# Own staging buffers for two chunks' k and q, first-layer weights fetched in pairs and held back, and new priorities, in a planned attention and MLP kernel

## The chip, the cores and the metric

The kernel runs on one core of one Trainium2 chip. The metric is the device time of one execution in microseconds (us). Three runs of the kernel before gave 1087.58, 1088.27 and 1089.88 us, a median of 1088.27 us.

## What is computed

The reference runs a delta-rule linear attention over 768 tokens (4 batches, 8 heads, head size 48), and sends its output, as 3072 tokens of 384 values, through two MLP layers with 2048 hidden units each:

```python
    for t in range(S):
        kt, vt, bt = (k_n[:, :, t], v[:, :, t], beta[:, :, t, None])
        y[:, :, t] = np.einsum('bhd,bhde->bhe', q[:, :, t], state)
        v_old = np.einsum('bhde,bhd->bhe', state, kt)
        state = state + bt[:, :, :, None] * np.einsum('bhd,bhe->bhde', kt, vt - v_old)
...
    h = x @ w_in          # layer 1: 0 below -1, h above 1, (h+1)^2/4 between; layer 2: h*clip(h+3,0,6)/6
    return (g @ w_out).astype(np.float32)
```

The MLP weights arrive as 64-bit floats, and the kernel must turn them into 32-bit ones.

## The kernel before

**Attention.** The 768 tokens are cut into 12 chunks of 64 (`c0` to `c11`). For each chunk `front(c)` loads k twice (`load_kv` into `KN`, `load_tok` into the staging tiles `ST0` and `ST1`), q (`load_tok`) and v (`load_v` into `E`), normalises k (`norms`), transposes k and q on TensorE through `ST` (`transposes`, L471), multiplies them (`products`), and inverts a triangular matrix for each head (`inverse`). The inverse is a chain of 15 small steps, each a multiply into `TMP` (L566) and a subtraction from `TL` (L571); in chunk 0 it runs on VectorE, in the others on GpSimd. Around the steps stand transposes on VectorE (L587 or L624 before, L604, L605, L620 and L633 behind) and four groups of 32x32 matmuls. `chain(c)` then takes the state through the chunk (matmuls `E,G`, then `E,KN`) and writes its output y (matmuls `KQ,E`), which is copied to `XB`; a last quarter of the rows goes by way of `YS` and six small DMAs (L786). Half `hb` 0 and half `hb` 1 of the heads are loaded and multiplied one after the other: with two staging tiles, the k and q of half 1 can be loaded only when the transposes of half 0 have read theirs.

**MLP.** Layer 1 works on blocks of tokens: chunk 0, chunk 1, and then pairs of chunks; layer 2 on six pairs. A block passes 16 slices `f` of the hidden units: 9 matmuls `XB,WL` (hidden values, called H here), an activation on ScalarE and VectorE (`GF`, `GH`, `GL`), and 9 matmuls `GH/GL,WL` (called O here). Values and weights are split into a high and a low part, hence three products each.

**Weights.** `wload` (L798) brings slice f: four DMAs of w_in and one of w_out, 768 KB in all, into one of four buffers `RAWL`, or for f 12 to 15 into a single `RAWR`. Then two halves (`pc` 0 and 1) are converted, each by three operations on VectorE (L826, L831, and the low part in L357), and by two or three on ScalarE (L366, L828, L366), into `WLA` or `WLB`. A buffer is loaded again once it has been read.

**The order.** Nothing is ordered by hand. `Plan` collects all operations with priorities from the table `PR`, and `emit` (L79) lays them out on the engines by its own estimate of durations; each engine then runs its list strictly in that order, and all DMAs are issued by SyncE (SP) in one list. A priority says which of several ready operations comes first. Up to the first MLP matmul, `emit` fills TensorE's free time with dummy matmuls (`bank<-GH`, 128x512; called fillers here):

```python
                while filling and x > filling:
                    d = 213.0 if is_warm(x) else 427.0
                    if x + d > t - 100.0:
                        break
```

Of the kernel before, what the change touches and what calls it, by code (L numbers as in the profile page):

```python
# [37 lines left out]
class Plan:  # L38
# [40 lines left out]
    def emit(self, banks, spare, fill):  # L79
# [54 lines left out]
        while todo:  # L134
# [3 lines left out]
            for e, lst in avail.items():  # L138
# [13 lines left out]
                for i in lst:  # L152
# [23 lines left out]
                if cand is not None and HOLD and e == "dve":  # L176
                    lim = cand[0] + HOLD
# [21 lines left out]
            if e == "pe":  # L199
# [70 lines left out]
def fused_kernel(  # L270
# [123 lines left out]
    P.op("act", 520, lambda: nc.scalar.activation(out=GH[0], in_=GF[0], func=AF.Copy, scale=1.0), r=[("gf", 0)], w=[("gh", 0)], prio=-30)  # L394
    for i in range(NST):
# [747 lines left out]
```

## Time and profile before

| | |
|---|---|
| median of three runs | 1088.27 us |
| the profiled execution: its time, and its span in the trace | 1090.76 us, 1089.0 us |
| TensorE matmuls (PE) busy | 1045.1 us, 96% |
| VectorE (DVE) busy | 662.6 us, 61% |
| ScalarE (ACT) busy | 595.7 us, 55% |
| GpSimd (POOL) busy | 277.6 us, 25% |
| granted TensorE clock, mean | 0.983 |

All rows below come from the one profiled execution, so sums are made against its 1090.76 us: its span and 1.76 us around it. PE's busy time holds the fillers and matmuls at the lower clock too, so 96% is not 96% of useful work. A granted clock of 1.00 is 2.4 GHz and 0.50 is 1.2 GHz.

### The profile page before, as it was taken

How to read it: one execution, taken by the hardware profiler on the slowest of the kernel's cores; microseconds unless marked ns; L12 is line 12 of the kernel's file. 1: busy time of each engine (PE TensorE's matmuls, PEld its weight loads, DVE VectorE, ACT ScalarE, POOL GpSimd, SP SyncE). 2: the span in 40 equal slices, each digit the busy share in tenths (PEclk: the TensorE clock that was granted, in tenths of full speed). 3: DMA queues.
4: the chain of work that ended last, by engine and by line, in shares of the span. 5: the costliest groups of instructions: out<-in, count | busy, mean ns of one | idle time of the engine just before them, and what ended most of it. 6: DMA issues, size and time to landing. Idle time of an engine off the chain costs nothing.

```text
span 1089.0 us, 25916 instructions
## 1 busy us (share of the span) xinstructions
PE 1045.1 (96%) x10684; PEld 890.1 (82%) x10684; DVE 662.6 (61%) x1258; ACT 595.7 (55%) x1164; POOL 277.6 (25%) x652
## 2 busy tenths in 40 slices
PE   8985899999999999999999999999999999999998
PEld 6764888887777778778778788898999998999897
DVE  4969778777869767786855589533333333333332
ACT  4768686766668576765755689433323232322322
POOL 3022313084755858548460000000000000000000
PEclk9987899999999999999999999999999999999999
DMA  9963243231314303322122284402011020200000
GB/s 179 191 142 66 61 99 66 45 63 36 59 21 97 69 17 59 90 45 46 40 57 83 80 257 139 116 1 88 1 41 47 1 87 2 59 29 1 29 1 29
DMA packets 174757, 71.86 MB, mean 66 GB/s; under 512 B 121264, under 2 KB 170544, under 8 KB 174640
## 3 DMA queue, kind: packets, MB, share of 16 engines
q1 hardware_dynamic: 174640, 70.22, 27.1%
q8 instruction: 84, 1.38, 0.6%
q14 instruction: 33, 0.27, 0.1%
HBM read 53.68 MB, written 14.16 MB: 62 GB/s over the span
## 4 chain that ended last, share of the span: by engine, by line
PE 72%; DVE 11%; ACT 5%; DMA 4%; POOL 3%; issue 3%; SPq 1%; DVEq 0%; POOLq 0%; ACTq 0%
PE bank L389 71%; DMA RAWL<-in_moe_w_in_dram 2%; DVE X L506 2%; POOL TL L571 1%; POOL TMP L566 1%; ACT KQ L514 1%; DVE GF L880 1%; PE bank L471 1%; DVE KQ L535 1%; DMA RAWR<-in_moe_w_in_dram 1%; DVE GL L357 1%; DVE DL L624 1%; ACT G L366 1%; SPq L815 1%; DVE XB L777 1%
## 5 line engine op out<-in xcount | busy, mean ns | idle before, releaser
L389 PE MATMUL bank<-XB,WLA 128*128 128x512 f32 (+1 forms) x1404 | 341.2, 386 | 13.4 <-DMA XB<-YS 7.1
L389 PEld LDWEIGHTS bank<-XB,WLA 128*128 128x128 f32 x1404 | 251.9, 193 | 62.1 <-ACT TBS L828 6.6
L357 DVE TENSOR_TENSOR GL<-GF,GH 128x512 fp32r<-128x512 f32 (+1 forms) x208 | 139.4, 671 | 82.9 <-PE bank L389 57.4
L884 DVE SCALAR_TENSOR_TENSOR GF<-GF,bank 128x512 f32<-128x512 f32 x96 | 66.1, 688 | 193.0 <-ACT GF L883 192.9
L366 ACT ACTIVATE GH<-GF 128x512 fp32r<-128x512 f32 (+1 forms) x202 | 120.9, 599 | 114.3 <-DVE GF L884 69.1
L883 ACT ACTIVATE GF<-bank 128x512 f32<-128x512 f32 x96 | 57.5, 599 | 204.5 <-PE bank L389 203.6
L566 POOL TENSOR_TENSOR TMP<-TL,DL 128x126 f32<-128x126 f32 (+25 forms) x293 | 113.0, 386 | 115.8 <-DVE DL L624 65.7
L571 POOL TENSOR_TENSOR TL<-TL,TMP 128x126 f32<-128x126 f32 (+25 forms) x293 | 126.6, 432 | 23.0
L389 PE MATMUL bank<-GH,WLA 128*128 128x512 f32 (+1 forms) x504 | 121.5, 373 | 2.6 <-DVE GH L368 1.5
L389 PE MATMUL bank<-XB,WLB 128*128 128x512 f32 (+1 forms) x468 | 112.4, 382 | 0.2 <-DVE GF L880 0.2
L389 PE MATMUL bank<-WLA,GH 128*128 128x384 f32 x576 | 112.3, 336 | 0.0
L389 PEld LDWEIGHTS bank<-WLA,GH 128*128 128x128 f32 x576 | 102.8, 188 | 6.4
L389 PEld LDWEIGHTS bank<-GH,WLA 128*128 128x128 f32 x504 | 85.9, 192 | 20.7 <-ACT GH L366 3.5
L389 PEld LDWEIGHTS bank<-XB,WLB 128*128 128x128 f32 x468 | 83.4, 191 | 15.5 <-DVE GF L880 0.4
L880 DVE SCALAR_TENSOR_TENSOR GF<-bank,GF 128x512 f32<-128x512 f32 (+1 forms) x112 | 68.6, 612 | 45.0 <-ACT GF L879 43.8
L878 ACT ACTIVATE GF<-bank 128x512 f32<-128x512 f32 (+1 forms) x112 | 59.8, 534 | 60.6 <-PE bank L389 56.1
L389 PE MATMUL bank<-GL,WLA 128*128 128x512 f32 (+1 forms) x252 | 65.9, 370 | 0.0
L879 ACT ACTIVATE GF<-GF 128x512 f32<-128x512 f32 (+1 forms) x112 | 63.5, 567 | 2.4
L389 PE MATMUL bank<-WLA,GL 128*128 128x384 f32 x288 | 61.5, 334 | 0.0
L389 PEld LDWEIGHTS bank<-WLA,GL 128*128 128x128 f32 x288 | 51.0, 188 | 0.0
L389 PE MATMUL bank<-GH 128*128 128x512 f32 x176 | 50.8, 437 | 0.0
L389 PEld LDWEIGHTS bank<-GL,WLA 128*128 128x128 f32 x252 | 43.9, 191 | 8.2 <-issue 0.3
(135 smaller groups left out, 1357.6 us busy)
## 6 DMA issues: line engine op xcount, KB each, us to landing
XB<-X SPq DMA_DIRECT2D x36, 256.0 KB, 4.7
X<-XB SPq DMA_DIRECT2D x30, 256.0 KB, 2.6
KN<-in_k_dram SPq DMA_DIRECT2D x24, 192.0 KB, 4.0
ST<-in_k_dram SPq DMA_DIRECT2D x48, 96.0 KB, 3.1
ST<-in_q_dram SPq DMA_DIRECT2D x48, 96.0 KB, 3.3
E<-in_v_dram SPq DMA_DIRECT2D x24, 192.0 KB, 3.8
RAWL<-in_moe_w_out_dram SPq DMA_DIRECT2D x12, 384.0 KB, 4.2
KQ<-in_moe_w_in_dram SPq DMA_DIRECT2D x12, 384.0 KB, 5.2
```

Source lines behind the costliest of these rows:

```text
L357: alts[e] = (d, lambda e=e: ENG[e].tensor_tensor(out=val(out), in0=val(in0), in1=val(in1), op=op))
L366: lambda: nc.scalar.activation(out=val(out), in_=val(in_), func=AF.Copy, scale=scale))
L389: nc.tensor.matmul(o, l, r, start=start, stop=stop)
L471: nc.tensor.transpose(bk.tile[0:112, p * 128:(p + 1) * 128], ST[i][:, p, 0:112], IDN)
L506: P.op("dve", 335, lambda bk=bk, u0=u0, rr=rr, ro=ro: nc.vector.tensor_tensor(out=X[rr, u0:u0 + NP, :], in0=bk.tile[ro].rearrange("p (a x) ...
L566: P.op(te, d, lambda t=t, s=s, r0=r0, a0=a0, a1=a1, m=m: ve.tensor_tensor(out=t[:, a0:a1], in0=TL[:, r0 + a0:r0 + a1, s:s + 1].to_broadcas ...
L571: P.op(te, d, lambda t=t, s=s, r0=r0, a0=a0, a1=a1: ve.tensor_tensor(out=TL[:, r0 + a0:r0 + a1, 0:s], in0=TL[:, r0 + a0:r0 + a1, 0:s], in1 ...
L878: P.op("act", da, lambda: nc.scalar.activation(out=gf, in_=ps, func=AF.Relu, scale=0.5, bias=0.5), r=[hkey(hb)], w=[gk], prio=MP)
L879: P.op("act", da + 48, lambda: nc.scalar.activation(out=gf, in_=gf, func=AF.Square), w=[gk], r=[gk], prio=MP)
L880: P.op("dve", 1.06 * n + 60, lambda: nc.vector.scalar_tensor_tensor(out=gf, in0=ps, scalar=1.0, in1=gf, op0=ALU.max, op1=ALU.min), r=[hkey ...
L883: P.op("act", da, lambda: nc.scalar.activation(out=gf, in_=ps, func=AF.Relu, scale=1.0 / 6.0, bias=0.5), r=[hkey(hb)], w=[gk], prio=MP)
L884: P.op("dve", 1.06 * n + 60, lambda: nc.vector.scalar_tensor_tensor(out=gf, in0=gf, scalar=1.0, in1=ps, op0=ALU.min, op1=ALU.mult), r=[hke ...
```

## The change

- **Staging.** The list `ST` gets four more entries, which are not new tiles but parts of `G0` and `G1`, the tiles that hold the inverse. Half 1 of chunk 0 uses the two in `G0`, half 1 of chunk 1 the two in `G1`, and half 0 of both uses `ST0` and `ST1`. From chunk 2 on there are two as before. The four parts are zeroed first; the zeroing of `G` for its later use (`zero_g`) moves behind the products of chunks 0 and 1.
- **Weights.** `wload` takes a list of slices. The first twelve of layer 1 come in pairs: the same five DMAs move 1536 KB, with runs twice as long in w_in, into one of two buffers that are each as large as two were. A pair's buffer is free once both slices are converted. Slices 12 to 15 and layer 2 stay single.
- **Held back.** DMAs of layer 1's weights are marked `bulk`: the planner places one no earlier than 2.5 us before its own estimate of when the DMA engines are free.
- **The planner's numbers.** Seven priorities, a bias and a margin change; a filler counts 228 or 430 ns instead of 213 or 427, and must end 150 ns ahead of the next matmul instead of 100; short runs of a DMA count as more bytes.

```diff
-PR = dict(kv=-2.451, tok=-1.879, norm=-2.407, tr=-1.803, prod=-3.087, pm=-1.495, inv=-2.162, sv=-0.287, w=-1.124, chain=-0.022, y=-0.474,
-          wl=-0.036, wls=0.003, mp=0, lv=-0.894, first=3.58, bias=27.418, fill=3000, tpool=tuple(range(1, 12)), hc=2, halves=1, biasa=601.736, b16=(0, 1, 2, 3), hyst=4058, margin=800, umargin=300, urg=('inv', 's'), sw=(217, 95), ad=('act', 'dve'), dp=('dve', 'pool'), dg=('dve',), dw=('dve',), pq=190)
+PR = dict(kv=-2.566, tok=-1.879, norm=-2.601, tr=-1.803, prod=-3.087, pm=-0.932, inv=-2.162, sv=0.06, w=-1.449, chain=-0.205, y=-0.455,
+          wl=-0.036, wls=0.003, mp=0, lv=-0.894, first=3.58, bias=-148.421, fill=3000, tpool=tuple(range(1, 12)), hc=2, halves=1,
+          biasa=601.736, b16=tuple(range(0, 4)), hyst=4058, fgap=150, back=2500.0, dh=0, margin=753.154, umargin=300, urg=('inv', 's'),
...
+                    if o["bulk"]:
+                        t = max(t, dma_free - PR["back"])
...
+    gs = [G[i].rearrange("p u e s -> p (u e s)") for i in range(2)]
+    extra = [gs[0][:, 0:512], gs[0][:, 512:1024], gs[1][:, 1024:1536], gs[1][:, 1536:2048]]
+    ST += [x.rearrange("p (a x) -> p a x", a=NP) for x in extra]
...
-        i = stage[0] % NST
+        if c < 2:
+            i = (0 if hb == 0 else 2 + 2 * c) + stage[0] % 2
+        else:
+            i = stage[0] % NST
...
-    def wload(f, wi, wo, perm, prio, raw, rkey, tmps):
+    def wload(fs, wi, wo, perm, prio, raw, rkey, tmps):
...
+        if c < 2:
+            zero_g(c)
...
+    rawp = RAWL.rearrange("p (g i) c -> p g (i c)", i=2)
+    for g in range(NFA // 2):
+        wload([2 * g, 2 * g + 1], w1i, w1o, True, PR["wl"] + PR["wls"] * 2 * g, rawp[:, g % 2, :], ("raw", g % 2), tmps1)
```

What this does to the engines' lists shows in three places. The first is SP's list near the start, before; `KN`, `ST` and `E` are the k, q and v of chunks 0 and 1, `RAWL` the weights, and the two `ST` rows at the end are half 1 of chunk 0.

```order
L422 DMA KN_76<-in_k_dram 64x16x48 x2
L411 DMA ST_78<-in_k_dram 64x8x48 x2
L411 DMA ST_79<-in_q_dram 64x8x48 x2
L429 DMA E_71<-in_v_dram 64x16x48 x2
L422 DMA KN_77<-in_k_dram 64x16x48 x2
L815 DMA RAWL<-in_moe_w_in_dram 48x3x256
L815 DMA RAWL<-in_moe_w_in_dram 16x3x256
L815 DMA RAWL<-in_moe_w_in_dram 48x3x256
L815 DMA RAWL<-in_moe_w_in_dram 16x3x256
L411 DMA ST_78<-in_k_dram 64x8x48 x2
L411 DMA ST_79<-in_q_dram 64x8x48 x2
```

In the changed kernel there follow on the k and q of half 0 and the first half of v:

```order
L420 DMA G_74<-in_k_dram 64x8x48 x2
L420 DMA G_74<-in_q_dram 64x8x48 x2
L438 DMA E_71<-in_v_dram 64x16x48
L431 DMA KN_77<-in_k_dram 64x16x48 x2
L420 DMA ST_78<-in_k_dram 64x8x48 x2
L420 DMA G_75<-in_k_dram 64x8x48
L420 DMA ST_79<-in_q_dram 64x8x48 x2
L420 DMA G_75<-in_k_dram 64x8x48
L420 DMA G_75<-in_q_dram 64x8x48 x2
L438 DMA E_72<-in_v_dram 64x16x48 x2
L420 DMA ST_78<-in_k_dram 64x8x48 x2
L420 DMA ST_79<-in_q_dram 64x8x48 x2
```

Half 1 of chunk 0 (the first two rows, with `G`) now comes right behind half 0; the rest of chunk 1 and half 0 of chunk 2 (the last two `ST` rows) follow, and the next row is the first weight. The first DMA of a weight was the 16th on SP and is the 34th. Further on, the five DMAs of the fourth pair stand ahead of the six `XB<-YS` of chunk 0, and the fifth pair behind them.

The second place is VectorE at the start of chunk 0's inverse: `DL`, `TL` and `TMP` belong to the inverse, `TBS` and `WLA` to the conversion of weights, `X<-KN` to the norms of chunk 1. Before:

```order
L587 STREAM_TRANSPOSE DL<-X 128x512
L357 TENSOR_TENSOR WLA<-TBS,WLA 128x384
L593 TENSOR_SCALAR DL<-DL,PAR 128x256
L831 SCALAR_TENSOR_TENSOR TBS<-TBS 128x384
L595 SCALAR_TENSOR_TENSOR DL<-DL,PAR 128x256
L368 CAST WLA<-TBS 128x384
L566 TENSOR_TENSOR TMP<-TL,DL 128x15
L357 TENSOR_TENSOR X<-KN_77 128x768
L571 TENSOR_TENSOR TL<-TL,TMP 128x15
L357 TENSOR_TENSOR WLA<-TBS,WLA 128x384
L566 TENSOR_TENSOR TMP<-TL,DL 128x28
```

and now:

```order
L596 STREAM_TRANSPOSE DL<-X 128x512
L602 TENSOR_SCALAR DL<-DL,PAR 128x256
L604 SCALAR_TENSOR_TENSOR DL<-DL,PAR 128x256
L360 TENSOR_TENSOR X<-KN_77 128x768
L575 TENSOR_TENSOR TMP<-TL,DL 128x15
L452 TENSOR_REDUCE SM<-X 128x16
L580 TENSOR_TENSOR TL<-TL,TMP 128x15
L454 TENSOR_SCALAR SM<-SM 128x16
L575 TENSOR_TENSOR TMP<-TL,DL 128x28
L580 TENSOR_TENSOR TL<-TL,TMP 128x2x14
L575 TENSOR_TENSOR TMP<-TL,DL 128x39
```

From the transposition into `DL` up to the next one into `NH` (L605, now L614), VectorE had 20 operations of weight conversion (seven L831, seven into `WLA`, six L826) and has four now (one, one and two); the scaling of v (`E<-E,NRM`) stands there twice instead of once, since GpSimd did one. From `NH` to the last subtraction for `YS` it had 24 and has 31.

The third place is TensorE between the first 32x32 matmuls of chunk 0's inverse and the first matmul of the state chain; the rows 128x512 are fillers. Before:

```order
L389 MATMUL bank_100<-GH_69 128x512 x9
L389 MATMUL bank_98<-NH,GF_66 32x32 x64
L389 MATMUL bank_100<-GH_69 128x512 x4
L389 MATMUL bank_99<-DL,NH 32x32 x64
L389 MATMUL bank_100<-GH_69 128x512 x7
L471 MATMUL bank_101<-IDN,ST_79 112x128 x4
L389 MATMUL bank_102<-NH,LT 32x32 x32
L389 MATMUL bank_100<-GH_69 128x512 x7
L389 MATMUL bank_103<-DL,NH 32x32 x32
L389 MATMUL bank_100<-GH_69 128x512 x7
L389 MATMUL bank_96<-E_71,G_74 64x48 x16
```

and now:

```order
L392 MATMUL bank_100<-GH_69 128x512 x27
L392 MATMUL bank_98<-NH,GF_66 32x32 x64
L480 MATMUL bank_99<-IDN,ST_79 112x128 x4
L392 MATMUL bank_100<-GH_69 128x512
L392 MATMUL bank_101<-DL,NH 32x32 x64
L392 MATMUL bank_100<-GH_69 128x512 x4
L392 MATMUL bank_102<-NH,LT 32x32 x32
L392 MATMUL bank_100<-GH_69 128x512 x3
L392 MATMUL bank_103<-DL,NH 32x32 x32
L392 MATMUL bank_100<-GH_69 128x512 x3
L392 MATMUL bank_96<-E_71,G_74 64x48 x16
```

The fillers between the four groups of 32x32 matmuls became 1, 4, 3 and 3 instead of 4, 7, 7 and 7, and three more behind `E,G` went. Up to the first of these groups there are 103 fillers instead of 148: the largest part that went is the 25 between the products of half 0 and the transposes of half 1, now 2. In all there are 114 fillers instead of 176. The first matmul of layer 1 is still the one behind both y of chunk 0. In block 0 the weights of slices 0 to 11 are still converted before `WLB`, and the count of matmuls of each kind is the same.

## Rows read from the trace of the kernel before

**Rows 1.** The page, part 1: busy time of each engine.
```profile
PE 1045.1 (96%) x10684; PEld 890.1 (82%) x10684; DVE 662.6 (61%) x1258; ACT 595.7 (55%) x1164; POOL 277.6 (25%) x652
```
**Rows 2.** Windows: stretch, length, busy PE, PEld, DVE, ACT, POOL, clock, DMA, GB/s.
```profile
0.00:56.40 56.40, 49.38 (x332) 38.20 (x333) 39.64 (x109) 36.70 (x74) 12.74 (x23) 1.00 0.92 184
56.40:87.10 30.70, 21.01 (x609) 16.95 (x609) 21.07 (x47) 18.76 (x40) 9.70 (x32) 0.87 0.65 139
87.10:122.00 34.90, 25.09 (x534) 21.74 (x538) 29.36 (x71) 27.95 (x61) 2.49 (x4) 0.73 0.30 66
122.00:236.00 114.00, 108.17 (x2207) 100.33 (x2199) 91.03 (x201) 81.64 (x194) 38.44 (x106) 0.96 0.31 63
236.00:625.00 389.00, 382.17 (x4759) 303.77 (x4759) 286.00 (x505) 253.32 (x483) 214.19 (x489) 1.00 0.26 57
625.00:1089.00 464.00, 459.33 (x2265) 409.13 (x2263) 195.53 (x330) 177.29 (x316) 0.00 (x0) 1.00 0.18 55
```
**Rows 3.** Waits of TensorE: for whom, us in total, times, longest.
```profile
PE bank L389 <- DMA XB<-YS: 7.1, 2, 6.4
```
**Rows 4.** Timeline of TensorE: start, us, instructions [idle before <- releaser].
```profile
15.35 5.97 PE L389 MATMUL bank<-GH 128*128 128x512 f32 x25
21.16 0.60 PE L471 MATMUL bank<-IDN,ST 128*112 128x128 f32 x4
...
24.22 1.10 PE L389 MATMUL bank<-KQ 48*64 48x128 f32 x32
...
56.37 1.46 PE L389 MATMUL bank<-NH,GF 32*32 32x32 f32 x128
...
62.45 3.17 PE L389 MATMUL bank<-GH 128*128 128x512 f32 x7
...
79.56 1.06 PE L389 MATMUL bank<-KQ,E 64*48 64x64 f32 x32
87.06 1.16 PE L389 MATMUL bank<-XB,WLA 128*128 128x256 f32 x2 [6.45 <-DMA XB<-YS]
88.92 3.75 PE L389 MATMUL bank<-XB,WLA 128*128 128x256 f32 x16 [0.70 <-DMA XB<-YS]
```
**Rows 5.** Timeline of VectorE, chunk 0's inverse and output.
```profile
29.57 1.10 DVE L587 STREAM_TRANSPOSE DL<-X 128x512 f32<-128x512 f32 x1
...
55.61 0.71 DVE L605 STREAM_TRANSPOSE NH<-DL 128x512 f32<-128x512 f32 x1
...
83.32 0.29 DVE L770 TENSOR_TENSOR YS<-bank,YS 48x128 fp32r<-48x128 f32 x1 [0.55 <-ACT XB L366]
```
**Rows 6.** Groups by form on VectorE, 29.5 to 56.3 us: busy, mean ns.
```profile
L831 DVE SCALAR_TENSOR_TENSOR TBS<-TBS 128x384 int32<-128x384 int32 x7 | 3.8, 549 | 0.0
L357 DVE TENSOR_TENSOR WLA<-TBS,WLA 128x384 fp32r<-128x384 f32 x7 | 3.8, 539 | 0.0
...
L826 DVE TENSOR_SCALAR TBS<-RAWL 128x384 int32<-128x384 int32 x6 | 3.4, 565 | 0.0
...
L357 DVE TENSOR_TENSOR E<-E,NRM 64x768 f32<-64x768 f32 x1 | 1.0, 955 | 0.0
```
**Rows 7.** Timeline of SyncE's DMA issues.
```profile
13.55 1.28 SPq L411 DMA_DIRECT2D ST<-in_k_dram  x2
14.93 1.28 SPq L411 DMA_DIRECT2D ST<-in_q_dram  x2
...
82.80 3.98 SPq L786 DMA_DIRECT2D XB<-YS  x6
...
145.13 2.79 SPq L815 DMA_DIRECT2D RAWR<-in_moe_w_in_dram  x4
```
**Rows 8.** Timeline of TensorE, block 0 and block 1 of layer 1.
```profile
127.02 2.07 PE L389 MATMUL bank<-E,G 128*64 128x48 f32 x64
...
208.16 2.03 PE L389 MATMUL bank<-XB,WLA 128*128 128x256 f32 x15
```
**Rows 9.** Timeline of VectorE: the last conversion for `WLB`, slice 15.
```profile
162.98 0.49 DVE L357 TENSOR_TENSOR WLB<-TBS,WLB 128x384 fp32r<-128x384 f32 x1
```

More of the change, by code (lines that the diff above doesn't have):

```diff
@@ L175, in emit @@
                         cand = k
-                if cand is not None and HOLD and e == "dve":
-                    lim = cand[0] + HOLD
+                if cand is not None and PR["dh"] and e == "dve":
+                    lim = cand[0] + PR["dh"]
                     end = cand[0] + ops[cand[3]]["alts"][e][0]
@@ new lines, in wload @@
+            P.dma(lambda o=o, a=a: nc.sync.dma_start(out=o, in_=a), rows * KT, rows * 1024 * KT * (nf if i < len(parts) - 1 else KT),
+                  w=[rkey + (i,)], pre=[rkey], prio=prio, bulk=perm)
+        v3 = lambda ap: ap.rearrange("p (a c) -> p a c", a=KT)
+        for k, f in enumerate(fs):
+            P.tag = f"wl f{f} {perm}"
+            for pc in range(2):
+                n = wcount[0]
+                wcount[0] += 1
+                tk, sk = ("tb", n % 2), ("sx", n % 2)
+                tb, s_ = tmps[n % 2]
+                sl = (DM * pc, DM * pc + DM)
+                if pc == 0:
+                    hl = ri[:, :, 256 * k:256 * k + 256].rearrange("p a (c t) -> p t a c", t=2)
+                else:
+                    hl = ro[:, k, :].rearrange("p (a c t) -> p t a c", a=KT, t=2)
+                lw, hw = hl[:, 0], hl[:, 1]
+                need = [rkey] + [rkey + (i,) for i in (range(len(parts) - 1) if pc == 0 else [len(parts) - 1])]
+                cpalt(AD, DM, v3(tb.bitcast(F32)), hw.bitcast(F32), False, 2.0 ** -112, r=need, w=[tk], prio=prio)
+                P.op("dve", 67 + 0.53 * DM, lambda s_=s_, hw=hw: V.tensor_scalar(
+                    out=v3(s_), in0=hw, scalar1=-2147483648, scalar2=None, op0=ALU.bitwise_and), r=need, w=[sk], prio=prio, port=("dve",))
+                P.op("act", 495, lambda s_=s_, lw=lw: nc.scalar.activation(
+                    out=s_.bitcast(I16).rearrange("p (a c t) -> p t a c", a=KT, t=2)[:, 0], in_=lw.bitcast(U32), func=AF.Relu, scale=0.875 * 2.0 ** -29, bias=0.49),
+                    r=need + [sk], w=[sk], prio=prio)
+                P.op("dve", 466, lambda tb=tb, s_=s_: V.scalar_tensor_tensor(
+                    out=tb, in0=tb, scalar=3, in1=s_, op0=ALU.logical_shift_left, op1=ALU.bitwise_or),
+                    r=[tk, sk], w=[tk], prio=prio, port=("dve",))
+                cpalt(AD, DM, lambda f=f, sl=sl: wl(f, 0, *sl), tb.bitcast(F32), False, r=[tk, ("wlb", f >= NFA)], w=[("w", f, pc, 0)], prio=prio)
+                ttalt(DW, DM, lambda f=f, sl=sl: wl(f, 1, *sl), tb.bitcast(F32), lambda f=f, sl=sl: wl(f, 0, *sl).bitcast(F32), ALU.subtract,
+                      r=[tk, ("w", f, pc, 0)], w=[("w", f, pc, 1)], prio=prio)
@@ L961, in fin2, with zero_g @@
                   r=[("eo", bi % 2, t)], prio=-1)
+    def zero_g(s_):
+        P.tag = ""
+        zk = [("zg", s_)] + [("gw", s_, hb, dl) for hb in range(2) for dl in range(2)] + tkeys(s_, 0) + tkeys(s_, 1) + \
+            [("st", 2 + 2 * s_ + i, b) for i in range(2) for b in range(2)]
+        zero(G[s_][32:64, :, 0, :], zk, 1200)
+        zero(G[s_][32:64, :, 1, 0:32], zk, 600)
+        zero(G[s_][96:128, :, 0, 0:32], zk, 600)
     def front(c):
@@ L995, in fused_kernel @@
         zero(KQ[32:64, PQi(s_, 0, 0):PQi(s_, U - 1, 0) + 1:2, :], [("zq", s_)] + [("qt", s_, hb, 0) for hb in range(2)], 1200)
[L996 to L1000 removed]
+    for i in range(4):
+        zero(ST[2 + i], [("st", 2 + i)] + ([("braw", 0), ("braw", 1)] if i >= 2 else []), 470)
     front(0)
```

65 lines of the change are left out of this document (19 added, 46 removed).

## The prediction

> **What bounds the kernel now.** I read the page's busy times first: TensorE is busy for 96% of the span [rows 1], so time can only come from where TensorE does not do useful work at full clock. The windows by stage show where that is [rows 2]. From 236 us on it is busy 841.5 of 853 us at a clock of 1.00: nothing in the change touches that part but small shifts of order. The loss lies ahead of it. Up to 87.06 us no MLP matmul runs at all [rows 4]; TensorE works through chunk 0's attention and 176 fillers, and at the end it waits 6.45 us for the DMAs that bring the last rows of chunk 0's output [rows 3, 4]. From 87.1 to 122 us it is busy 25.1 of 34.9 us at a granted clock of 0.73, while VectorE is busy 29.4 and ScalarE 28.0 us [rows 2]: there the two engines that convert weights and evacuate results set the pace. From 122 to 236 us TensorE is nearly full again, 108.2 of 114 us.
>
> So the question is how much earlier the first MLP matmul comes, and how much of that VectorE and ScalarE take back in block 0, because conversions that used to run in the first 87 us now run later.
>
> **The change, part by part.**
>
> *Staging and the order of loads.* The k and q of half 1 were issued at 13.55 us, behind chunk 1's k and four weight DMAs [rows 7], and transposed at 21.16 us, behind 25 fillers [rows 4]. Now they are issued right behind half 0's. A filler at full clock costs (21.16 - 15.35)/25 = 0.232 us, one at the low clock 3.17/7 = 0.45 us [rows 4]. From the first product to the second the list loses 22 fillers (34 to 12), 22 x 0.232 = 5.1 us; ahead of the first product it gains four at the low clock, at most 4 x 0.45 = 1.8 us, part of which lies in waiting for the first tokens. So the second product ends 3.3 to 5.1 us before 25.32 us; I take 4.2. The inverse's first transposition, at 29.57 us [rows 5], moves by the same 4.2 us, to 25.4.
>
> *Weights held back.* From 29.57 to 55.61 us VectorE is one dense stretch [rows 5], and chunk 0's inverse passes through it. By the order, 16 operations of conversion leave it: six L831, six into `WLA`, four L826. At 0.549, 0.539 and 0.565 us [rows 6] that is 3.3 + 3.2 + 2.3 = 8.8 us; one more scaling of v comes in, 0.96 us. Busy times of neighbours overlap, by about 0.08 us where rows follow each other, so 16 of them give back 1.3 us: 8.8 - 1.0 - 1.3 = 6.5 us. The bounds are 8 us, and 5, since the inverse's steps depend on each other and will wait where nothing stands between them any more. With 4.2 + 6.5 = 10.7 us the matmuls at 56.37 us [rows 4] come at 45.7 us. TensorE's list agrees: up to there it holds 45 fillers less, 45 x 0.232 = 10.4 us, so neither engine waits long for the other.
>
> *From there to the first MLP matmul* it took 87.06 - 56.37 = 30.7 us [rows 4]. Seventeen fillers go, 3.9 us at full clock and 7.7 at the low one. Against that stand seven more conversion operations on VectorE in this stretch, 7 x 0.47 = 3.3 us, which lie partly in its free time: it was busy 21.1 of 30.7 us [rows 2]. Bounds: 0 and 7 us. I take 3, nearest to the fillers at full clock, less a part of VectorE's extra work. The first MLP matmul then comes at 87.1 - 10.7 - 3.0 = 73.4 us, 13.7 us earlier. The wait of 6.45 us ahead of it stays: VectorE's last subtraction for `YS` (83.32 us, [rows 5]) and six DMAs of 0.66 us each [rows 7] are what it consists of, and neither changes.
>
> *Pairs.* A pair has the same five DMA issues as a slice before, so SP issues 30 DMAs for twelve slices instead of 60; at some 0.65 us each [rows 7] SP gains 20 us, which lie beside other work, because SP waits for buffers anyway. The bytes are the same. In 0 to 56.4 us the DMA engines were 92% busy at 184 GB/s [rows 2], so 1536 KB need about 8 us. With a pair to a buffer, a pair's load (8 us) and its conversion, 4 halves of about 1.5 us (a row of each of the three VectorE groups, [rows 6]), take 14 us for a buffer, and two buffers give four slices in 14 us. Block 0 had its last slice converted at 163.5 us [rows 9], sixteen slices in 76 us or 4.8 us a slice, so loads have room. Cost: 0, hidden beside block 0; without that cover it is the second rival.
>
> The Trainium skill ("DMA: Bandwidth & Descriptors", section Bandwidth) asks for DMAs of at least 1 MiB for most of the peak rate, and calls those under 64 KB bound by descriptors. A w_out part of a pair, 768 KB, comes nearer to that than 384 KB; by the page's rate for 1 MB, 341 GB/s, a pair would take about 4.6 us (an estimate), while the row gives 184 GB/s with 92% of the engines taken. I stay with the row; by the page the sum would be the same and the second rival less likely.
>
> *Block 0.* Between the first y copies of chunk 0 and those of chunk 1 VectorE's list grows by 15 operations, most of them conversions: some 5.8 us at the rates above. Before, VectorE had 5.5 us free in 87 to 122 us and 23 us free in 122 to 236 us [rows 2]. In exchange about 18 MLP matmuls (2.4 us at 2.03/15 = 0.135 us each, [rows 8]) now stand ahead of the state matmuls of chunk 1 that came at 127.02 us [rows 8], so TensorE has more to do meanwhile. Bounds: a loss of 5.8 us, a gain of 3. I take 0.
>
> *The rest* (new priorities, margin of 753 ns): from 236 us on TensorE idles 11.5 us [rows 2], 4.7 of them behind 625 us, in layer 2; the list there keeps its shape. 0, with 2 us to either side.
>
> *Sum:* 13.7 us off the profiled 1090.76 us is 1077.1 us. The median of the runs is 2.5 us below the profiled run, so I forecast 1074.5 us.
>
> **The rivals.**
>
> *Block 0 gives some back.* VectorE and ScalarE were at 84% and 80% in 87 to 122 us [rows 2]; with 5.8 us more, TensorE waits for activations. And slices 12 to 15 still pass one buffer. The last conversion of slice 15 ended at 163.5 us [rows 9], its DMAs issued at 145.13 us [rows 7]; these now stand behind the output DMAs of chunk 1 and the conversion of slice 14. The place decides if slice 15 is ready less than 13.7 us earlier than before. Each us of lateness is a us of TensorE. Price 4 to 9 us: 1078.5 to 1083.5, say 1080.5.
>
> *Block 0 gains too.* From 87 to 236 us TensorE idled 15.6 us and ran at the low clock for a part [rows 2]. If the longer list of ready MLP work and c1's earlier inverse close a third, 5 us more go: 1069.5. For it: weights are no longer converted ahead of the first inverse, so attention of chunks 1 and 2 is further on when block 0 starts. Against it: the two converting engines are the limit there.
>
> *The clock stays down, slower than before.* At the low clock 16 matmuls of 256 columns took 3.75 us, 0.234 each, and at full clock 0.135 [rows 4, 8]. Block 0 has 288. Before, TensorE was back at full clock soon after 122 us, with some 80 of them done [rows 2]. If the sparser start holds the low level for all of block 0, the other 207 cost 0.10 us more each, 20.5 us: 1095. It decides the sign when 137 more of them run cold. For it: in 87 to 122 us the clock was 0.73 with gaps like those that will come back. Against it: as soon as TensorE was filled, the clock rose to 0.96 in the mean. The Trainium skill ("TensorE: Matmul & The Clock Gate", Part 1) says that the low clock is the default and activity lifts it, which is the rule that speaks against taking fillers out; the clock of 1.00 in the filled stretch to 56.4 us [rows 2] agrees.
>
> *SP holds the output back.* The fourth pair's five DMAs stand ahead of the six `XB<-YS` on SP and wait until slices 2 and 3 are converted. If that is later than the output is ready, the first MLP matmul comes later by as much. By the order the last conversion of slice 3 stands some thirty VectorE operations ahead of the output, 10 us or more at 0.3 to 0.5 us each. For the gain to vanish it would have to slip by 24 us: 1086 to 1089, about as before. That the change does less than it says lies here too.
>
> **How the numbers follow.** Forecast (1071 to 1078): 0.55. Block 0 gives back: 0.22. Block 0 gains: 0.15. SP holds the output: 0.04. Clock: 0.04. The two last are outside the range; it takes in the forecast, the give-back up to 1082 and the gain down to 1067, which is 8 in 10. Faster by over 0.2% (2.2 us, about what a measurement of this kernel can tell from no change), that is below 1086.1: 0.92. Within: 0.03. Slower: 0.05.
>
> **What would show it.** In the changed profile: half 1's transposes near 17 us and the first 32x32 matmuls near 45.7 us (steps one and two); the first `XB,WLA` matmul at 73.4 us, still behind a wait of some 6 us for `XB<-YS` (step three); the state matmuls of chunk 1 at 111 to 115 us, and the last conversion of slice 15 near 150 us instead of 163.5 (block 0 neutral); layer 2 again some 460 us long. Wrong would be: a first MLP matmul later than 78 us, waits of TensorE or VectorE for `RAWL` or `RAWR` of several us, or a clock under 0.8 beyond 115 us.

## The result: slower, by 0.6%

The changed kernel takes 1096.22 us (median of 5 runs, 1093.50 to 1098.82), the kernel before 1088.27 us (1087.13 to 1089.88) beside it: a ratio of 1.0061, 95% interval 1.0035 to 1.0087. It is slower, where I had forecast 1074.5 us; the time lies outside the range. The profiled execution has a span of 1094.4 us against 1089.0.

Timeline of TensorE in the changed kernel, which answers to [rows 4] (start, us, instructions, idle time before them and what ended it):

```profile
45.97 1.29 PE L392 MATMUL bank<-NH,GF 32*32 32x32 f32 x128 [1.64 <-DVE NH L614]
...
48.65 0.67 PE L392 MATMUL bank<-DL,NH 32*32 32x32 f32 x55 [0.58 <-ACT NH L369]
54.05 1.19 PE L392 MATMUL bank<-DL,NH 32*32 32x32 f32 x73 [4.73 <-issue]
55.17 2.08 PE L392 MATMUL bank<-GH 128*128 128x512 f32 x4
57.18 1.59 PE L392 MATMUL bank<-NH,LT 32*32 32x32 f32 x51
62.45 0.54 PE L392 MATMUL bank<-NH,LT 32*32 32x32 f32 x13 [3.68 <-issue]
...
75.81 0.76 PE L392 MATMUL bank<-KQ,E 64*48 64x64 f32 x20 [1.08 <-issue]
84.98 3.72 PE L392 MATMUL bank<-XB,WLA 128*128 128x256 f32 x12 [8.41 <-ACT WLA L369]
...
97.75 1.01 PE L392 MATMUL bank<-XB,WLA 128*128 128x256 f32 x3 [4.15 <-DVE GF L899]
```

The first 32x32 matmuls come at 45.97 us instead of 56.37, as forecast (45.7). Then two groups of the inverse's matmuls, 128 and 64 operations that belong together, are cut in two: TensorE stands still for 4.73 and 3.68 us in the middle of a group and the profile names nothing it waited for ("issue"). With the third such gap that is 9.5 us. Before, the same stretch had two, together 3.2 us:

```profile
61.13 1.39 PE L389 MATMUL bank<-DL,NH 32*32 32x32 f32 x116 [1.77 <-issue]
...
71.44 0.31 PE L389 MATMUL bank<-DL,NH 32*32 32x32 f32 x6 [1.39 <-issue]
```

Of the 10.4 us gained at 46 us, 4.0 are left when the last product of y ends (76.57 us; before 79.56 + 1.06 = 80.62, [rows 4]), and 2.1 at the first MLP matmul (84.98 against 87.06).

Windows of the changed kernel, which answer to [rows 2] (same columns):

```profile
46.00:56.00 10.00, 4.68 (x263) 4.07 (x264) 4.68 (x11) 4.96 (x10) 0.00 (x0) 0.86 1.10 226
56.00:66.00 10.00, 6.32 (x126) 4.63 (x127) 6.08 (x14) 5.74 (x11) 0.31 (x1) 0.50 0.44 109
...
87.00:122.00 35.00, 26.27 (x515) 23.44 (x518) 30.23 (x70) 27.89 (x61) 2.38 (x4) 0.50 0.50 109
122.00:236.00 114.00, 105.15 (x2191) 96.67 (x2184) 93.70 (x200) 82.73 (x196) 38.21 (x105) 0.97 0.32 66
236.00:625.00 389.00, 381.51 (x4772) 303.44 (x4772) 282.08 (x499) 250.70 (x484) 211.27 (x489) 1.00 0.26 56
```

Beside the first gap the DMA engines are taken to 1.10 of their time. While TensorE stands, VectorE (busy 4.7 of 10 us) and ScalarE (5.0) stand with it: VectorE waits 5.05 us for TensorE's product, and ScalarE's next operation reads what VectorE then writes. From 87 to 122 us the granted clock is 0.50, the lower of its two levels (1.2 GHz), where it was 0.73 before; TensorE is busy longer and does less. From 122 to 236 us it idles 3 us more than before; from 236 to 625 us the two kernels differ by 0.7 us.

SyncE's DMA issues in the changed kernel ([rows 7] are those of before):

```profile
39.98 2.04 SPq L827 DMA_DIRECT2D RAWL<-in_moe_w_in_dram  x4
42.07 0.42 SPq L827 DMA_DIRECT2D RAWL<-in_moe_w_out_dram  x1
42.54 2.37 SPq L827 DMA_DIRECT2D RAWR<-in_moe_w_in_dram  x4
45.19 0.35 SPq L827 DMA_DIRECT2D RAWR<-in_moe_w_out_dram  x1
...
50.24 2.77 SPq L827 DMA_DIRECT2D RAWL<-in_moe_w_in_dram  x4
...
80.67 4.00 SPq L795 DMA_DIRECT2D XB<-YS  x6
```

Between 39.98 and 45.5 us it issues the second pair and slice 12, 1536 and 768 KB; at 179 GB/s from 40 to 46 us and 226 from 46 to 56 they need 11 to 12 us, so the queues are full when TensorE's products arrive at 46 to 54 us. The third pair follows at 50.24.

### The profile page after: what moved, and what is told of

It reads as the page before. It is cut to its first block, busy times and chain, and to the rows that moved or that the text cites. A ratio compares the mean times of both kernels' runs of the same rounds, so it can differ in the third digit from the quotient of the medians.

```text
span 1094.4 us, 25705 instructions
## 1 busy us (share of the span) xinstructions
PE 1036.4 (95%) x10622; PEld 882.0 (81%) x10622; DVE 665.4 (61%) x1252; ACT 597.9 (55%) x1173; POOL 274.0 (25%) x654
## 3 DMA queue, kind: packets, MB, share of 16 engines
q8 instruction: 83, 1.36, 0.5%
## 4 chain that ended last, share of the span: by engine, by line
PE 74%; DVE 9%; ACT 5%; issue 2%; DMA 1%; DVEq 0%; ACTq 0%
PE bank L392 73%; DVE GF L899 1%; ACT XB L369 1%; DVE XB L786 1%; DVE X L515 1%; ACT GH L369 1%; ACT KQ L523 1%; PE bank L480 1%; ACT G L369 1%; DVE YS L779 1%; DVE TBS L845 0%; DVE KQ L544 0%; ACT YS L369 0%; DVE X L360 0%; DVE GL L360 0%
## 5 line engine op out<-in xcount | busy, mean ns | idle before, releaser
L360 DVE TENSOR_TENSOR GL<-GF,GH 128x512 fp32r<-128x512 f32 (+1 forms) x208 | 136.6, 658 | 84.9 <-PE bank L392 57.1
L575 POOL TENSOR_TENSOR TMP<-TL,DL 128x126 f32<-128x126 f32 (+25 forms) x293 | 115.5, 394 | 132.3 <-DVE DL L633 86.0
L580 POOL TENSOR_TENSOR TL<-TL,TMP 128x126 f32<-128x126 f32 (+25 forms) x293 | 120.1, 410 | 23.0
L523 ACT ACTIVATE KQ<-bank 64x256 f32<-64x256 f32 x92 | 34.8, 378 | 21.9 <-DVE X L515 16.5
```

Of the source, the lines that this page charges most:

```text
L360: alts[e] = (d, lambda e=e: ENG[e].tensor_tensor(out=val(out), in0=val(in0), in1=val(in1), op=op))
L523: alts = {"act": (285, lambda o=o, pin=pin: nc.scalar.activation(out=o, in_=pin(), func=AF.Copy, scale=1.0))}
L575: P.op(te, d, lambda t=t, s=s, r0=r0, a0=a0, a1=a1, m=m: ve.tensor_tensor(out=t[:, a0:a1], in0=TL[:, r0 + a0:r0 + a1, s:s + 1].to_broadcas ...
L580: P.op(te, d, lambda t=t, s=s, r0=r0, a0=a0, a1=a1: ve.tensor_tensor(out=TL[:, r0 + a0:r0 + a1, 0:s], in0=TL[:, r0 + a0:r0 + a1, 0:s], in1 ...
```

## The experiments

Theory A: the gaps on issue come from the weight bytes in the DMA queues beside the inverse's matmuls, and they are what the change lost. Against it: B, the gaps belong to the order of the instructions; C, the low clock is the loss; D, block 0 goes by VectorE and ScalarE; and that the new numbers or the pairs as such are to blame. All ratios are to the kernel before on the same chip; its median there was 1088.3 to 1091.0 us, so runs from different chips are better compared by ratio than by median. "Gaps" is the sum of TensorE's waits that end on issue from 46 us to the end of y.

| run | what differs from the changed kernel | gaps us | first MLP us | median us | ratio (95%) |
|---|---|---|---|---|---|
| changed | | 9.5 | 84.98 | 1096.22 | 1.0061 (1.0035-1.0087) |
| e1 | fewer bytes | 1.3 | 77.47 | 1087.10 | 0.9991 (0.9974-1.0008) |
| e2 | 18 fillers more | 9.9 | 86.59 | 1092.95 | 1.0045 (1.0025-1.0066) |
| e3 | staging only | 3.0 | 82.05 | 1094.73 | 1.0057 (1.0030-1.0083) |
| e4 | old numbers | 8.0 | 85.49 | 1094.13 | 1.0055 (1.0032-1.0078) |
| e5 | SyncE: two moves | 3.5 | 77.74 | 1087.37 | 0.9984 (0.9966-1.0002) |
| e6 | SyncE: one move | 6.2 | 81.08 | 1090.27 | 1.0007 (0.9982-1.0031) |
| e7 | not held back | 3.8 | 77.98 | 1088.96 | 0.9988 (0.9966-1.0010) |
| e8 | single slices | 3.0 | 76.85 | 1084.28 | 0.9947 (0.9926-0.9969) |
| e9 | pairs issued in halves | 3.8 | 80.67 | 1087.93 | 0.9976 (0.9959-0.9993) |
| e10 | e8 and 18 fillers | 1.8 | 76.79 | 1085.19 | 0.9952 (0.9933-0.9972) |
| e11 | e8, slice 12 late | 2.7 | 77.03 | 1082.46 | 0.9930 (0.9903-0.9956) |
| e12 | single slices, not held back | 1.4 | 71.91 | 1082.91 | 0.9923 (0.9894-0.9952) |
| e13 | before with new numbers | 1.8 | 88.53 | 1095.82 | 1.0063 (1.0043-1.0084) |
| e14 | e12, evictions late | 3.0 | 74.02 | 1084.12 | 0.9935 (0.9910-0.9961) |
| e15 | e12 again | 3.4 | 74.58 | 1083.87 | 0.9943 (0.9922-0.9965) |

**Fewer bytes, same order (e1).** The order of all engines stays (two fills of buffers on VectorE in the first 5.7 us are added, so that nothing unwritten is read). By `KT` = 3 a third of w_in moves, not the sixth that the expectation names.

```diff
-P.dma(lambda o=o, a=a: nc.sync.dma_start(out=o, in_=a),
+cut = perm and fs[0] in (2, 4, 12)
+P.dma(lambda o=o, a=a, cut=cut: nc.sync.dma_start(
+    out=o[:, 0:1] if cut else o, in_=a[:, 0:1] if cut else a),
...
```

> The changed kernel, word for word in its order, but of the transfers of slices 2, 3, 4, 5 and 12 only a sixth (w_in) or a part of it moves (w_out: one slice of a pair, of slice 12 nothing is left out), so some weights are wrong numbers and their products with them. Theory A (TensorE's gaps that end on nothing but issue, 4.73 us at 49.3 and 3.68 us at 58.8, come from the weight transfers that run beside them at a DMA share over 1): the gaps together fall from 9.5 us to about 3 us, y's last product ends near 70 instead of 76.6, the first product of the MLP starts near 80, time 1090 to 1093. Rival B (the gaps belong to the order of the instructions, not to the transfers): gaps still 8 us or more, y's end at 76 to 77, time 1095 to 1097.

Of 9.5 us of gaps 1.3 are left, and with the rest go 8 to 9 us (1087.10), more than expected. A holds, B falls: the same instructions in the same order have 1.3 us of gaps when fewer bytes move beside them.

**Same bytes at other places (e5, e6).** Only SyncE's list differs; all other engines' lists are word for word those of the changed kernel, and everything is computed.

```diff
+self.move("wl f12 True", "wl f6 True")   # e5, e6: slice 12 behind slices 6 and 7
+self.move("wl f2 True", "wl f0 True")    # e5 only: slices 2, 3 behind 0, 1
 for i in self.order:
     self.ops[i]["fn"]()
```

> The changed kernel with every engine's order as it is, but for SyncE's: the transfers of slices 2 and 3 are issued right behind those of slices 0 and 1 (near 31 us instead of 40) and those of slice 12, which nobody reads before 100 us, behind slices 6 and 7 (near 68 us instead of 42.5). All is computed. Theory A (gaps on issue come from the weight bytes that move beside the 32x32 products): the gap of 4.7 us shrinks to under 2, the gaps together to 2 to 6 us, first product of the MLP at 78 to 82, time 1088 to 1092. Rival B (gaps belong to the order of instructions): gaps 8 us or more, time 1095 to 1097.

> The changed kernel in which only slice 12's transfers (768 KB) move on SyncE, from 42.5 us to behind slices 6 and 7. Theory A: half the effect of the run with both moves: gaps together 5 to 8 us, first product of the MLP at 81 to 84, time 1091 to 1094. Rival B: no change, 1095 to 1097.

Timeline of TensorE in e5:

```profile
46.08 1.29 PE L400 MATMUL bank<-NH,GF 32*32 32x32 f32 x128 [1.66 <-DVE NH L622]
...
50.43 0.94 PE L400 MATMUL bank<-DL,NH 32*32 32x32 f32 x73 [0.21 <-issue]
...
55.25 0.38 PE L400 MATMUL bank<-NH,LT 32*32 32x32 f32 x13 [1.00 <-issue]
...
70.05 0.76 PE L400 MATMUL bank<-KQ,E 64*48 64x64 f32 x20 [2.29 <-issue]
77.74 3.72 PE L400 MATMUL bank<-XB,WLA 128*128 128x256 f32 x12 [6.92 <-ACT WLA L377]
```

The gaps stand at the same instructions (before the last 73, 13 and 20 of their groups) and only their length differs: the place belongs to TensorE's list, the length to the transfers. The DMA view of the stretch in which the changed kernel has its first gap, 49.3 to 54.05 us (busy tenths, rate, and the queues with their packets, MB and share), of the changed kernel and then of e5:

```profile
DMA  9999999899989999997989999999999999999978
...
q1 hardware_dynamic: 1484, 0.95, 113.3%
```

```profile
DMA  0000000000002489963647995966789998979897
...
q1 hardware_dynamic: 1250, 0.56, 59.6%
```

Where the queues stand empty at 49 us TensorE goes on after 0.21 us; where they are full it waits 4.73. What it waits for shows on another queue, q8, of a kind that the profile calls "instruction". One packet of 16 KB moves on it from 51.42 to 52.63 us in the changed kernel, among full queues, and from 47.55 to 48.95 us in e5, nearly alone and while TensorE still works. The view of 51.4 to 52.7 us of the changed kernel, and then that of 47.5 to 49 us of e5:

```profile
DMA  9966969667999789986989999999999999999999
...
q8 instruction: 1, 0.02, 5.8%
```

```profile
DMA  2911111111111111000000000000000000000000
...
q8 instruction: 1, 0.02, 5.8%
```

TensorE goes on at 54.05 and at 50.43 us, 1.4 and 1.5 us behind the end of its packet. Other waits go the same way: in the profiles of both kernels and of all fifteen runs there are 35 waits on issue of 0.2 us or more between 46 us and the end of y, and each ends 1.2 to 1.9 us behind the end of a packet on q8.

The places fit too. Counted from the first matmul, they lie behind matmuls 471 to 473, 599 or 600, 728, and 854 or 855, in every list, in steps of about 128. The rows above show one step: 73 + 4 + 51 = 128 matmuls from gap to gap. In all, 83 packets move for the changed kernel's 10622 matmuls, 128 to a packet; with their weight loads that is 256 instructions to 16 KB, or 64 bytes each (an estimate).

So the gaps are waits for the next piece of TensorE's program. No view names that as the releaser, and no run changes the fetching itself; the packets' times and places leave little else. That the lengths hang on the weight transfers is shown by e1 and e5. When the packet is asked for is not shown. Of 44 later waits on issue in the same profiles, up to 1000 us, four fit neither rule (2.1 us in e4, 3.9 to 4.6 us near 145 us in e8, e10 and e11), and their cause is open.

The run with one move lies between (6.2 us of gaps, 1090.27 us). From the changed kernel by way of e6 to e5 the first MLP matmul comes 7.2 us earlier and the median falls by 8.9 (8.4 by the ratios). Both times are 0.6 to 0.7 us below what theory A had expected.

The Trainium skill ("Trainium Architecture — The Big Picture", section The software stack) has the instruction streams brought to the engines by DMA when a program is loaded. That section speaks of the load alone; in the trace the 83 packets, 1.36 MB, move while the kernel runs.

**The clock (e2, e10).** 18 fillers more ahead of the first MLP matmul, in the changed kernel and in e8.

```diff
+if extra and self.ops[i]["eng"] == "pe" and self.ops[i]["prio"] >= MLP:
+    for _ in range(extra):   # 18
+        self.fill()
+    extra = 0
```

> The changed kernel with 18 more fillers (128x512 products that nobody reads) on TensorE just ahead of the first product of the MLP, where it waited 8.4 us. Theory C (the low granted clock, 0.50 from 86 to 116 us against 0.67 before, is what is lost behind 85 us, and it is low because TensorE stood idle): clock from 87 to 122 us at 0.7 or more, the products of the MLP in block 0 at 0.14 to 0.2 us each, time 1091 to 1093. Rival D (block 0 goes by VectorE's and ScalarE's backlog, the clock only follows): clock higher but time within 1.5 us of the changed kernel, 1095 to 1098.

> The run with single slices (1084.3 us), with 18 fillers more on TensorE ahead of the first product of the MLP, where it waits 8.0 us. Theory C (the low clock, 0.50 in the stretch from 76 to 87 us, costs time): clock over 0.8 there, first products of the MLP at 0.14 us each instead of 0.29, time 1080 to 1083. Rival D (block 0 goes by VectorE and ScalarE): clock higher, time 1083.5 to 1086.

Windows of e2, and then of e10 around the start of block 0:

```profile
76.00:87.00 11.00, 5.82 (x53) 4.31 (x45) 8.62 (x18) 8.85 (x19) 5.68 (x20) 0.99 0.50 88
87.00:122.00 35.00, 24.58 (x498) 21.53 (x502) 31.67 (x74) 29.34 (x64) 2.38 (x4) 0.60 0.52 112
```

```profile
66.00:76.00 10.00, 6.95 (x146) 5.79 (x144) 7.42 (x18) 8.28 (x18) 8.20 (x24) 1.00 0.63 115
76.00:87.00 11.00, 6.75 (x155) 6.02 (x159) 10.35 (x25) 9.74 (x20) 1.21 (x4) 0.51 0.87 216
```

The fillers lift the clock ahead of block 0, but in block 0 it falls again, while TensorE is busy 6.75 of 11 us (e10). From 87 to 122 us it is 0.60 in e2 against 0.50, short of the 0.7 that C had asked for. The times don't move clearly: e10 against e8 0.9952 to 0.9947, e2 against the changed kernel 1.0045 to 1.0061 with overlapping intervals (e2's 1092.95 us is in C's range, not in D's). Fillers ahead of block 0 bring nothing that can be told from noise. What a high clock inside block 0 would be worth was not tried, so C as such stays open.

**Which part of the change does it (e3, e4, e7, e8, e12, e13, e15).** The planner orders all engines anew in each of these, so they price whole plans.

```diff
 # e8, e12, e15: one slice to a buffer, as before
-for g in range(NFA // 2):
-    wload([2 * g, 2 * g + 1], w1i, w1o, True, PR["wl"] + PR["wls"] * 2 * g, rawp[:, g % 2, :], ("raw", g % 2), tmps1)
+for f in range(NF):
+    wload([f], w1i, w1o, True, PR["wl"] + PR["wls"] * f, RAWL[:, i, :] if f < NFA else RAWR, ("raw", i), tmps1)
 # e3, e7, e12, e15: nothing held back
-back=2500.0
+back=1e9
 # e3, e4: old numbers;  e3 with single slices;  e13: before with the new ones
-kv=-2.566, norm=-2.601, pm=-0.932, sv=0.06, w=-1.449, chain=-0.205, y=-0.455, bias=-148.421, margin=753.154, fgap=150
+kv=-2.451, norm=-2.407, pm=-1.495, sv=-0.287, w=-1.124, chain=-0.022, y=-0.474, bias=27.418, margin=800, fgap=100
...
```

> The kernel before with the staging buffers alone: slices one by one, no holding back, the old numbers for priorities, costs and fillers. If the staging gives what the prediction's steps 1 and 2 said and the rest of the change loses it: first 32x32 products near 46, first product of the MLP at 73 to 79, time 1076 to 1083. If the gain is lost even so (later work bounds block 0): first product of the MLP at 80 or later, time 1086 to 1090.

> The changed kernel (staging, pairs, transfers held back) with the old numbers for priorities, costs and fillers. If the new numbers lose the gain: 1078 to 1088, with 1.5 us or less of waits in the stretch from 300 to 500 us. If the pairs lose it: gaps on issue of 8 us or more between 46 and 76 us again, time 1092 to 1098.

> The changed kernel without the holding back of layer 1's transfers (the planner's other rules and numbers unchanged, so orders move on all engines). If the holding back is what piles the weight transfers up at 40 to 60 us: the weights start near 22 us, gaps on issue together under 5 us, first product of the MLP at 76 to 82, time 1086 to 1091. If not: gaps as in the changed kernel, time 1093 to 1098.

> The changed kernel with the pairs undone: slices one by one in four buffers, 384 KB and less to a transfer, same bytes. If the size of the paired transfers makes the gaps: under 4 us of gaps, time 1086 to 1091. If it is the bytes, whatever their pieces: gaps 6 us or more, time 1092 to 1098.

> The run with single slices without the holding back (the planner orders all engines anew). If the holding back is worth something without the pairs: gaps 4 us or more, time 1086 to 1092. If the order of the transfers matters only where pairs pile them up: within 2 us of 1084.3.

> The kernel before with the new numbers for priorities, costs and fillers alone: no staging buffers, single slices, nothing held back. Against the run with staging, single slices, new numbers and nothing held back (ratio 0.9923) it prices the staging. If the staging is worth what steps 1 and 2 of the prediction said: first 32x32 products at 54 to 58 us, ratio 1.000 to 1.006. If the new numbers alone bring the gain: ratio under 0.995.

> The run with staging, single slices, new numbers and nothing held back once more, beside the one with the evictions moved: 1081 to 1084 us, ratio 0.990 to 0.995.

As a table of ratios:

| | old numbers | new numbers |
|---|---|---|
| before's loads | 1 | 1.0063 (e13) |
| staging | 1.0057 (e3) | 0.9923, 0.9943 (e12, e15) |
| staging, held back | | 0.9947 (e8) |
| staging, pairs | | 0.9988 (e7) |
| staging, pairs, held back | 1.0055 (e4) | 1.0061 (changed) |

Staging alone makes the kernel slower and the new numbers alone do too; together, without pairs, they are 6 to 8 us faster. Beside the new numbers the staging is worth 13 to 15 us (e13 against e15 and e12). Three of these runs missed their ranges: e3 came out 4.7 us above the upper one, with its first 32x32 matmuls at 49.46 us instead of 46; e8 is 1.7 us faster than expected; in e13 the first 32x32 matmuls, at 59.01 us, and the ratio lie just past theirs. The pairs cost 5 to 7 us without the holding back and 12 with it (e8 against the changed kernel). The holding back costs 8 us with pairs; without them its price, 0.0004 to 0.0024 of the time, is inside the intervals. e8 and e12 are faster than both kernels.

e3's loss sits elsewhere than that of the changed kernel. It starts block 0 at 82.05 us, 5 us early, and then loses it; its window and, behind it, that of e12:

```profile
122.00:236.00 114.00, 98.69 (x2042) 91.40 (x2041) 88.25 (x194) 74.19 (x175) 40.43 (x110) 0.93 0.35 67
```

```profile
122.00:236.00 114.00, 101.52 (x2046) 92.04 (x2037) 90.31 (x197) 79.44 (x185) 42.25 (x117) 0.99 0.35 69
```

TensorE is busy 98.7 of 114 us there, against 108.2 before [rows 2], with waits of 4.6 us for activations (`GF`), 3.4 us for the state's sums and 2.2 us for a step of an inverse. That the old numbers order this stretch badly for the earlier start is read from these waits and not tried by a run. e12 idles there too, but it has done more by 122 us (33.5 of 35 us busy from 87 us on).

e8 moved more bytes beside the inverse than the changed kernel and had a third of its gaps. The DMA view from 46 to 64 us of the changed kernel and of e8 (last number: median us from issue to landing):

```profile
DMA packets 2637, 3.35 MB, mean 186 GB/s; under 512 B 1240, under 2 KB 1624, under 8 KB 2633
...
RAWL<-in_moe_w_out_dram SPq DMA_DIRECT2D x1, 768.0 KB, 9.0
```

```profile
DMA packets 4606, 3.89 MB, mean 216 GB/s; under 512 B 2451, under 2 KB 4000, under 8 KB 4602
...
RAWL<-in_moe_w_out_dram SPq DMA_DIRECT2D x3, 384.0 KB, 3.7
```

So it is not the bytes of a stretch alone. The pair's transfer lands 9.0 us after its issue, those of single slices after 3.7, which points to how much stands queued at the moment when TensorE's packet has to pass.

In e7 the gaps moved rather than went: its first MLP matmul comes at 77.98 us, and then this row stands among TensorE's waits from 87 to 236 us:

```profile
PE bank L392 <- issue: 8.8, 4, 5.0
```

e12 has 1.7 us there. e12 and e15 are one kernel, and their gap at matmul 473 was 1.43 us in one profiled execution and 3.08 in the other: the lengths vary from run to run.

**Size or depth (e9), and slice 12 once more (e11).**

```diff
 # e9, for the parts of a pair
+for h in range(2):
+    nc.sync.dma_start(out=o[:, :, 256 * h:256 * h + 256], in_=a[:, :, 256 * h:256 * h + 256])
 # e11: e8 and
+self.move("wl f12 True", "wl f7 True")
```

> The changed kernel in which each transfer of a pair is issued as two of half its size, one slice each, right behind each other; all orders else are the same, SyncE spends twice the time to issue them. Theory E (what holds the instruction fetch up is the weight bytes that stand in the queues at that moment, 2.3 MB issued from 40 to 45.5 us at some 210 GB/s, however they are cut): gaps together 6 to 10 us, time 1092 to 1097. Rival F (a transfer of 768 KB holds the queues longer than two of 384 KB): gaps under 4 us, time 1085 to 1090.

> The run with single slices, with slice 12's transfers moved on SyncE from 44 to 51 us to behind slice 7 (near 61 us), nothing else. If the bytes in the queue at 50 and 56 us still make its two gaps of 1.3 and 1.7 us: gaps together under 1.5 us, first product of the MLP near 75.5, time 1082 to 1083.5. If the remaining gaps are the cost of a fetch as such: gaps 2.5 to 3.5 us, time 1084 to 1085.

e9 went as F said (3.8 us, 1087.93 us), against E's bound. But it doesn't tell the two apart: issuing ten DMAs took SyncE 4.9 us for the second pair instead of 2.5, so fewer bytes stood queued as well. Whole pairs with short gaps (e5) show that large transfers alone don't make long ones. e11 leaves its question open: its gaps, 1.95 and 0.75 us, are those of the second reading (2.5 to 3.5 us together), its 1082.46 us is the time of the first, its first MLP matmul (77.03 us) fits neither, and its interval overlaps that of e8.

**From y's end to its ship (e14).** In the changed kernel the six DMAs start 4.1 us behind the last product of y (76.57 to 80.67), before 2.2. ScalarE and, behind it, VectorE show why:

```profile
76.11 1.97 ACT L369 ACTIVATE E<-bank 48x384 f32<-48x384 f32 x4
78.09 0.55 ACT L369 ACTIVATE YS<-bank 48x128 fp32r<-48x128 f32 x2
```

```profile
78.68 0.55 DVE L371 CAST XB<-bank 48x384 fp32r<-48x384 f32 x1 [1.04 <-ACT YS L369]
79.26 0.55 DVE L786 TENSOR_TENSOR XB<-bank,XB 48x384 fp32r<-48x384 f32 x1
80.36 0.61 DVE L779 TENSOR_TENSOR YS<-bank,YS 48x128 fp32r<-48x128 f32 x2 [0.55 <-ACT XB L369]
```

Four evictions of the state stand ahead of the copies of y's second half (before, one), and two operations for `XB` and a wait for ScalarE ahead of VectorE's subtractions for `YS`, for which the ship waits. The evictions are the smaller part: the copies start 1.5 us behind y's end instead of 1.1, but from there to the ship it takes 2.6 us instead of 1.1. From the ship's issue to the first MLP matmul it takes 4.3 us in both kernels (82.80 to 87.06 and 80.67 to 84.98), in e1 and in e5 as well, so it looks as if the ship sets this start and the `WLA` that the timeline names ends at about the same moment (84.91 us). e14 is e12 with:

```diff
+ev = [i for i in self.order if self.ops[i]["eng"] == "act" and self.ops[i]["tag"] == "chain c0"]
+# put behind the last ScalarE operation of "chain c0 h1 y"
```

> The run with staging, single slices, new numbers and nothing held back, with ScalarE's four evictions of the state (1.97 us) moved behind its copies of y's second half; every other engine's order as it was. If they hold up y and what ships it (before, one of them stood there, and the ship came 2.2 us behind y's end instead of 4.1): ship near 66 instead of 67.6, first product of the MLP near 70.3, and if the start of block 0 still carries to the end, 1 to 2 us less than the unmoved order beside it; if block 0 is held by VectorE and ScalarE further on, the same time within 0.7 us.

The copies come 2.2 us sooner behind y's end than in e15, but VectorE's list has conversions ahead of the subtractions, so the time from y's end to the ship falls only from 3.5 us (e15) to 2.6. The ship itself comes at 69.75 us, not near 66, since y ends later in this execution (67.19 us) than in e12's. The median stays: 1084.12 against 1083.87 us. One us at that place does not reach the end of this plan. Its window suggests what holds:

```profile
87.00:122.00 35.00, 32.18 (x588) 28.90 (x588) 32.64 (x81) 33.30 (x78) 5.06 (x9) 0.72 0.27 64
```

VectorE is busy 93% and ScalarE 95% there, as D had it.

## Why the prediction was wrong, step by step

- **Staging, the second product 4.2 us earlier: right, and somewhat more.** Half 1's transposes start at 14.39 us (forecast: near 17), its second product ends at 20.2 us (21.1), 5.2 us earlier than before and just past the bound of 5.1; the inverse's first transposition starts at 23.63 us (25.4).
- **Six and a half us out of VectorE's stretch: right only in the sum, by luck.** The first 32x32 matmuls come at 45.97 us against 45.7. But the inverse began 1.8 us earlier than forecast, and from there it took 22.3 us where the forecast had 20.3: two errors of about 2 us cancel.
- **Minus 3 us from there to the first MLP matmul: this step failed.** The stretch took 39.0 us, not 27.7. Of the 8.3 us over the 30.7 of before, the gaps on issue are 6.3 (9.5 less 3.2) and the way from y's end to the ship 1.9 (4.1 less 2.2). Without the gaps it takes 21.1 us from the first 32x32 matmul to the end of y in both kernels, so the 17 fillers that went, taken as time that comes free, gave nothing back. The gaps of 1.77 and 1.39 us stood in the trace of before, and the sum has no line for them. The only wait that it carries over is the one ahead of the first MLP matmul, which was to stay at 6.45 us since neither the subtraction for `YS` nor the six DMAs changed; it became 8.41, because that subtraction stands further back in VectorE's list. The rival that SP holds the output back did not come: the fourth pair's DMAs are out by 67.8 us, and the ship waits for VectorE.
- **Pairs at cost 0: wrong, and the largest error.** I asked whether the conversion would wait for the weights, which it hardly did, and not who else uses the queues that the weights fill. Undoing them is worth 12 us (e8, with all engines ordered anew); issuing the second pair and slice 12 elsewhere 8.9 (e5). One transfer of 768 KB, half a pair, landed 9.0 us after its issue, where the forecast had about 8 us for a whole pair. The Trainium skill ("DMA: Bandwidth & Descriptors", section Bandwidth) asks for large DMAs, and that pointed the wrong way here; its rate gave 4.6 us for a pair (an estimate).
- **Weights held back, counted as a gain alone: wrong with pairs.** I counted what leaves the first stretch and not where it arrives: from 40 us on, beside the inverse that had just been moved there. 7 to 8 us by e7, whose plan orders all engines anew.
- **Block 0 at 0: the rival was nearer.** From the first MLP matmul to the end the changed kernel takes 1009.4 us, before 1001.9; e5, with short gaps, 1007.2. The 5.3 us lie inside the 4 to 9 of the rival "block 0 gives some back". Slice 15, at which the rival was to decide, is converted at 171.08 us in the changed kernel (row below), 8.1 us later than before [rows 9] and 21 later than my mark of 150; in e5 at 161.26, 1.7 us earlier though its block 0 starts 9.3 us earlier. The state matmuls of chunk 1 came at 127.17 us, where 111 to 115 were forecast and 127.02 stood [rows 8]; in e5 at 117.54.

Timeline of VectorE in the changed kernel, the last conversion of slice 15:

```profile
171.08 0.56 DVE L360 TENSOR_TENSOR WLB<-TBS,WLB 128x384 fp32r<-128x384 f32 x1
```

- **The rest, new numbers at 0: wrong in both directions.** They cost 6.9 us on the kernel before and gain 12 to 15 us on the staged one with single slices (e3 against e12 and e15).
- **The clock rival gave the right time (1095) for another reason.** The clock did fall to 0.50, but behind the gaps (in e5, with short ones, it is 0.79 from 87 to 122 us), and it was at 1.00 again from 126 us on, not low through block 0; fillers ahead of block 0 brought nothing.

In sum, of the 21.7 us between forecast and result 8.9 go with where SyncE issues one pair and slice 12 (changed kernel against e5, which has 6.0 us less of gaps and starts the MLP 7.2 us earlier), 4.3 are the start of e5 behind 73.4 us, and 5.3 its way from there to the end. The remaining 3 us are the step from the profiled execution to the median: the forecast took 2.5 us off for it, and e5's median lies 0.5 us above its profiled execution. Open is how the loss behind the start divides between VectorE, ScalarE and the clock.

## What to carry to other kernels

Before moving bulk loads, look for waits on issue in the timeline of the engine with the longest instruction list, count whether they come a fixed number of instructions apart, and set them beside the packets of the instruction queues. Keep deep bursts of transfers away from stretches of many short instructions. A transfer that hides beside work can still hold up whatever else has to be fetched; here single slices left gaps no longer than those of before (3.0 us against 3.2). Numbers tuned for one plan are no property of the change: price a structural change with numbers fitted to it, and each number change with its structure.

## What was unexpected on the chip

- TensorE stopped for up to 5.0 us (e7, at 85 to 90 us) in the middle of a group of matmuls without any wait in its list. The stops lie multiples of about 128 matmuls apart and end 1.2 to 1.9 us behind a 16 KB packet of an instruction queue; at one such place they lasted 0.21 to 4.73 us, by what stood in the DMA queues.
- Transfers of 768 KB landed 9.0 us after their issue and such of 384 KB after 3.7, in the same stretch of two plans, so twice the size took 2.4 times as long; how much of it is size and how much the queue ahead of it, e9 doesn't separate.
- 216 GB/s of single slices beside the inverse did less harm than 186 GB/s of pairs.
